# wq in four strided transfers, output in four transfers, x loaded later, filler matmuls, and GpSimd closing: a change at the two ends of a stream-bound decode kernel

## The chip, the cores and the metric

The kernel runs on one core of a Trainium2 chip. Times are device microseconds (us) of that core. "Before" was timed again beside every kernel, on the same chip.

The span of a profile, from the first to the last instruction, is 1.8 us shorter than the time of the same execution (988.36 us against 990.17).

## The reference

Decode attention with a cache of 4096 keys, followed by a gated feed-forward network:

```
x: (4, 1, 640) bf16
k_cache, v_cache: (4, 32, 4096, 192)       201 MB each: nearly all the bytes
h   = x + Attn(layernorm(x)) @ wo          q = layernorm(x) @ wq, wq: (640, 6144)
out = h + (silu(ln(h) @ w_gate) * (ln(h) @ w_up)) @ w_down
```

## The kernel before

SyncE (SP) issues all the loads, from one queue: wq first, then the k and v slots in turn as slots come free, then wo, w_gate, w_up and w_down. An issue is the instruction by which an engine's queue starts a transfer; a transfer has landed with the last update of its semaphore that the trace shows (the 16th for wq here). The parts that matter here are the first and the last instructions (cuts marked with `...`):

```python
xd = dma("act", lambda e: e.dma_start(x16[:, :], x[:, 0, :].rearrange("b (n d) -> (b n) d", n=4)), S_x)
...
wq_land = dma("sp", lambda e: e.dma_start(            # 128 partitions x 61,440 B
    wqsb[:, :, :].rearrange("q c n -> q (c n)"), wq[:, :].rearrange("(q c) n -> q (c n)", c=CD)), S_wq)
...
load_k(0); load_k(1)
for u in range(NU):
    load_v(u)
    if u + 2 < NU: load_k(u + 2)
...
for c in range(CF):                                   # w_down, three transfers: c 0-5, 6-9, 10-11
    for n in range(4):
        a = op("pe", lambda e, c=c, n=n: e.matmul(
            psH[32 * n:32 * n + 32, 0:DQ], lhsT=guT[:, c, :], rhs=wdsb[:, c, n * DQ:(n + 1) * DQ],
            start=False, stop=(c == CF - 1), skip_group_check=True), [gut, wd_land[c], ln2])
a = op("dve", lambda e: e.tensor_copy(out=outsb[:, 0:DQ], in_=psH[:, 0:DQ]), [a])
fin = [dma(eng, lambda e, n=n: e.dma_start(           # two transfers of 8 rows of 320 B
    out[:, 0, n * DQ:(n + 2) * DQ].rearrange("b (n d) -> n b d", n=2),
    outsb[32 * n:32 * n + 64:RB, 0:DQ]), S_out, [a]) for n, eng in ((0, "sp"), (2, "act"))]
with nc.Block(no_gpsimd_drain=True) as block:
    pr.emit(block, "act", fin[-1:])                   # ACT waits for both
```

The result sits in 16 of 128 partitions, every eighth one (`RB` is 8).

## Time and profile before

| | before |
|---|---|
| time, median of 6 | 990.44 us (990.21 to 990.85) |
| span of the profile | 988.4 us |
| read from memory | 424.29 MB, 429 GB/s over the span |
| first bulk packets of the 16 DMA engines | 1.76 to 3.21 us, mean 2.22 |
| last w_down piece landed | 985.01 us (its first engine 983.36) |
| output issue starts, output landed, end | 985.92, 987.88, 988.36 us |

From the page of before: its span, the granted TensorE clock and DMA share in 40 slices (tenths, 9 is 90% or more), GB/s by slice, the bytes, and the chain of waits.

```profile
span 988.4 us, 9462 instructions
...
PEclk9788778887777888777788777778877778877776
DMA  9999999999999999999999999999999999999997
GB/s 403 426 440 424 438 436 428 436 430 436 436 428 438 430 434 436 428 438 432 432 436 428 438 432 432 436 428 438 432 432 436 428 438 434 430 436 428 440 429 327
...
HBM read 424.29 MB, written 0.01 MB: 429 GB/s over the span
## 4 chain that ended last, share of the span: by engine, by line
DMA 67%; PE 18%; DVE 12%; issue 1%; SPq 1%; DVEq 0%
```

The DMA row is full in every slice but the last. In the packet records a row of 61,440 B takes 2.267 us on one DMA engine: 27.1 GB/s, 434 GB/s for 16. Only the first and last slices (403 and 327 GB/s) have anything to give.

In the timelines PE is TensorE, PEld its weight loads, DVE VectorE and ACT ScalarE; SPq and ACTq are the queues of SP and ACT, and x2 marks two instructions shown as one line. SP's timeline of before at the start (start, duration, queue, line, transfer):

```profile
0.74 0.39 SPq L331 DMA_DIRECT2D wq_sb<-in_A_wq_dram  x1
1.20 0.41 SPq L355 DMA_DIRECT2D k<-in_A_k_cache_dram  x1
```

The timeline of before at the end, all engines:

```profile
984.28 0.40 PEld L573 LDWEIGHTS pb<-wd_sb,guT 128*32 128x32 bf16 x16 [0.81 <-DMA wd_sb<-in_B_w_down_dram]
984.28 1.24 PE L573 MATMUL pb<-wd_sb,guT 128*32 128x160 bf16 x24 [0.49 <-DMA wd_sb<-in_B_w_down_dram]
985.06 0.14 PEld L573 LDWEIGHTS pb<-wd_sb,guT 128*32 128x32 bf16 x8 [0.38 <-DMA wd_sb<-in_B_w_down_dram]
985.57 0.33 DVE L576 CAST gu<-pb 128x160 bf16<-128x160 f32 x1 [2.86 <-PE pb L573]
985.92 0.68 SPq L577 DMA_DIRECT2D out_dram<-gu  x1
985.92 1.38 ACTq L577 DMA_DIRECT2D out_dram<-gu  x1
```

The last weights land at 985.01. Eight matmuls, a copy and two output issues follow, and the program ends 2.44 us after the output issue starts. Nothing is streamed in that tail (0 GB/s from 985 to 987 us), so whatever ends last there counts in full. The output issues last 0.68 us on SP and 1.38 on ACT.

### The profile page before, as it was taken

How to read it: one execution, taken by the hardware profiler on the slowest of the kernel's cores; microseconds unless marked ns; L12 is line 12 of the kernel's file. 1: busy time of each engine (PE TensorE's matmuls, PEld its weight loads, DVE VectorE, ACT ScalarE, POOL GpSimd, SP SyncE). 2: the span in 40 equal slices, each digit the busy share in tenths (PEclk: the TensorE clock that was granted, in tenths of full speed). 3: DMA queues.
4: the chain of work that ended last, by engine and by line, in shares of the span. 5: the costliest groups of instructions: out<-in, count | busy, mean ns of one | idle time of the engine just before them, and what ended most of it. 6: DMA issues, size and time to landing. Idle time of an engine off the chain costs nothing.

```text
span 988.4 us, 9462 instructions
## 1 busy us (share of the span) xinstructions
PE 581.5 (59%) x4409; PEld 128.6 (13%) x2941; DVE 552.6 (56%) x447; ACT 117.1 (12%) x376; POOL 3.6 (0%) x18
## 2 busy tenths in 40 slices
PE   1777555676555567545556654546765555675554
PEld 0001011111011111001111110111110111110023
DVE  1487545566655556655556665555666555566521
ACT  0311111100111110111111011111001111101120
POOL 1000000000000000000000000000000000000000
PEclk9788778887777888777788777778877778877776
DMA  9999999999999999999999999999999999999997
GB/s 403 426 440 424 438 436 428 436 430 436 436 428 438 430 434 436 428 438 432 432 436 428 438 432 432 436 428 438 432 432 436 428 438 434 430 436 428 440 429 327
DMA packets 10571, 424.39 MB, mean 429 GB/s; under 512 B 1220, under 2 KB 1220, under 8 KB 1732
## 3 DMA queue, kind: packets, MB, share of 16 engines
q1 hardware_dynamic: 10522, 424.29, 99.5%
q8 instruction: 5, 0.08, 0.0%
q10 hardware_dynamic: 42, 0.01, 0.0%
q14 instruction: 2, 0.02, 0.0%
HBM read 424.29 MB, written 0.01 MB: 429 GB/s over the span
## 4 chain that ended last, share of the span: by engine, by line
DMA 67%; PE 18%; DVE 12%; issue 1%; SPq 1%; DVEq 0%
DMA k<-in_A_k_cache_dram 64%; DVE prod L413 12%; PE pb L161 11%; PE pb L463 4%; DMA wd_sb<-in_B_w_down_dram 4%; PE pb L421 2%; SPq L366 0%; DVE sc L426 0%; PE pb L469 0%; DVEq L413 0%; SPq L392 0%; SPq L386 0%; PE pb L573 0%; PE pb L435 0%; SPq L331 0%
## 5 line engine op out<-in xcount | busy, mean ns | idle before, releaser
L413 DVE TENSOR_TENSOR prod<-k,qball 128x6144 f16<-128x6144 bf16 x128 | 426.4, 3352 | 220.1 <-DMA k<-in_A_k_cache_dram 220.1
L161 PE MATMUL pb<-prod,identH 128*128 128x512 f16 x1408 | 386.0, 431 | 0.0
L421 PE MATMUL pb<-prod,identH 128*128 128x512 f16 x128 | 57.9, 452 | 337.5 <-DVE prod L413 337.5
L426 DVE TENSOR_REDUCE sc<-pb 128x32 f32<-128x512 f32 x128 | 88.1, 688 | 108.7 <-PE pb L161 108.7
L478 ACT ACTIVATE otmp<-pb,minv 128x192 f32<-128x192 f32 x32 | 13.5, 421 | 649.1 <-PE pb L463 649.1
L421 PEld LDWEIGHTS pb<-prod,identH 128*128 128x128 f16 x128 | 13.2, 103 | 585.3 <-DVE prod L413 472.4
L463 PE MATMUL pb<-v,pbuf 128*8 128x384 bf16 x1984 | 86.0, 326 | 0.0
L454 ACT ACTIVATE pbuf<-sc,negM 32x128 bf16<-32x128 f32 x128 | 73.4, 574 | 4.9
L463 PEld LDWEIGHTS pb<-v,pbuf 128*8 128x8 bf16 x1984 | 45.4, 86 | 28.8
L482 DVE SCALAR_TENSOR_TENSOR orow<-pb,minv,otmp 128x192 f32<-128x192 f32 x32 | 13.4, 418 | 53.7 <-ACT otmp L478 53.7
L498 PEld LDWEIGHTS pb<-orow,here 128*128 128x128 f32 x256 | 33.5, 191 | 73.5 <-issue 71.1
L498 PE MATMUL pb<-orow,here 128*128 128x48 f32 x256 | 31.7, 267 | 1.1 <-DVE orow L482 1.1
L454 ACT ACTIVATION_READ_ACCUMULATOR pbuf<-sc,negM 32x1 f32 x128 | 31.8, 248 | 0.0
L448 ACT ACTIVATE negM<-pb 128x4 f32<-128x4 f32 x32 | 5.6, 174 | 160.2 <-PE pb L444 160.2
L469 PEld LDWEIGHTS pb<-lsb,headm 128*128 128x128 f32 x64 | 12.3, 194 | 74.8 <-issue 71.1
L444 PE MATMUL pb<-negMc,ones_row 1*128 1x4 f32 x64 | 12.2, 258 | 11.8 <-DVE negMc L439 11.8
L435 PE MATMUL pb<-identF,msb 128*1 128x128 f32 x64 | 12.1, 271 | 9.8 <-DVE msb L431 9.8
L439 DVE TENSOR_REDUCE negMc<-pb 1x4 f32<-1x128 f32 x32 | 8.9, 278 | 15.1 <-PE pb L435 15.1
L444 PEld LDWEIGHTS pb<-negMc,ones_row 1*128 1x128 f32 x64 | 9.4, 182 | 21.2 <-DVE negMc L439 21.2
L469 PE MATMUL pb<-lsb,headm 128*128 128x1 f32 x64 | 9.2, 213 | 2.7 <-ACT pbuf L454 2.7
L491 ACT ACTIVATE here<-place 128x131 f32 (+1 forms) x32 | 10.0, 312 | 0.9
L338 PE MATMUL pb<-wq_sb,lnT 128*32 128x384 bf16 x20 | 2.7, 520 | 12.1 <-DMA wq_sb<-in_A_wq_dram 12.1
(65 smaller groups left out, 91.1 us busy)
## 6 DMA issues: line engine op xcount, KB each, us to landing
k<-in_A_k_cache_dram SPq DMA_DIRECT2D x32, 6144.0 KB, 39.5
v<-in_A_v_cache_dram SPq DMA_DIRECT2D x31, 6144.0 KB, 25.5
wq_sb<-in_A_wq_dram SPq DMA_DIRECT2D x1, 7680.0 KB, 21.5
k<-in_A_v_cache_dram SPq DMA_DIRECT2D x1, 6144.0 KB, 39.8
wo_sb<-in_A_wo_dram SPq DMA_DIRECT2D x1, 5760.0 KB, 24.1
wo_sb<-in_A_wo_dram SPq DMA_DIRECT2D x1, 1920.0 KB, 26.1
wg_sb<-in_B_w_gate_dram SPq DMA_DIRECT2D x1, 1920.0 KB, 30.3
wu_sb<-in_B_w_up_dram SPq DMA_DIRECT2D x1, 1152.0 KB, 32.6
```

What stands on the lines that cost most here:

```text
L161: return e.add_instruction(mybir.InstMatmult(name=e.bass.get_next_instruction_name(), engine=mybir.EngineType.PE, start_tensor_calc=start, ...
L413: op("dve", lambda e: e.tensor_tensor(out=prod[BUF[k]][:, :, :], in0=kslot[u % 2][:, k * QT:(k + 1) * QT, :], in1=qball[:, bass.ds(u + pr. ...
L421: op("pe", lambda e, j=j: (e.matmul if j == 0 else partial(held_matmul, e))(psR[k][:, 0:QT * R], lhsT=identH[:, :], rhs=prod[BUF[k]][:, :, ...
L426: op("dve", lambda e: e.tensor_reduce(sc[u % 2][:, k * QT:(k + 1) * QT], psR[k][:, 0:QT * R].rearrange("q (t r) -> q t r", r=R), AX.X, ALU ...
L435: op("pe", lambda e: e.matmul(psS[0:1, XT], lhsT=msb[:, 0:1], rhs=identF[:, :], start=True, stop=True), [g("rmax", u), g("negM", u - 1), p ...
L444: op("pe", lambda e: e.matmul(psS[:, XB], lhsT=ones_row[0:1, :], rhs=negMc[0:1, :], start=True, stop=True), [g("hmax", u), g("negM", u - 1 ...
L454: op("act", lambda e, h=h, r=r: e.activation(out=pbuf[r, :, h], in_=sc[u % 2][r, :], func=ACTF.Exp, bias=negM[r, h:h + 1], scale=alpha, ac ...
L463: op("pe", lambda e, t=t, n=n: e.matmul(psO[32 * n:32 * n + 8, 0:2 * DH], lhsT=pbuf[:, t:t + 2, :].rearrange("q t m -> q (t m)"), rhs=vsrc ...
L469: op("pe", lambda e: e.matmul(psS[:, XL], lhsT=headm[:, :, :].rearrange("q r m -> q (r m)"), rhs=lsb[:, :], start=True, stop=True), [g("ex ...
L478: op("act", lambda e: e.activation(out=otmp[:, :], in_=psO[:, 0:DH], func=ACTF.Copy, scale=minv[:, 0:1]), [g("pv", u), g("minv", u), g("st ...
L482: op("dve", lambda e: e.scalar_tensor_tensor(out=orow[:, :], in0=psO[:, DH:2 * DH], scalar=minv[:, 1:2], in1=otmp[:, :], op0=ALU.mult, op1 ...
L498: op("pe", lambda e, i=i: e.matmul(psT[:, bass.ds(JW * at_unit(u)[0], JW)], lhsT=here[:, NI - 1 - i:NI - 1 - i + 128], rhs=orow[:, JW * i: ...
```

## The change

The intent was to give every DMA engine rows from the first issue (four transfers of every fourth partition), keep x's small load out of the way at the start, keep the TensorE clock up by filler matmuls, write the output by four plain transfers, and let idle GpSimd do the closing wait.

```diff
-    xd = dma("act", ..., S_x)
+    xd = dma("act", ..., S_x, [lambda: c2])               # c2: the identity is built
-    wq_land = dma("sp", lambda e: e.dma_start(
-        wqsb[:, :, :].rearrange("q c n -> q (c n)"), wq[:, :].rearrange("(q c) n -> q (c n)", c=CD)), S_wq)
+    for i in range(4):
+        wq_land = dma("sp", lambda e, i=i: e.dma_start(
+            wqsb[i:128:4, :, :].rearrange("q c n -> q (c n)"),
+            wq[:, :].rearrange("(q c) n -> q (c n)", c=CD)[i:128:4, :]), S_wq)
+    def idle(n):                                          # n matmuls 128x256 into an unused bank
...
+    idle(3) after w_gate, idle(2) inside w_up, idle(6) after w_up, idle(3) before w_down c = 6
-    fin = [... two transfers "n b d" of 8 rows, SP and ACT ...]
+    fin = [dma("sp" if n < 2 else "act", lambda e, n=n: e.dma_start(
+        out[:, 0, n * DQ:(n + 1) * DQ], outsb[32 * n:32 * n + 32:RB, 0:DQ]), S_out, [a]) for n in range(4)]
-        pr.emit(block, "act", fin[-1:])
+        pr.emit(block, "pool", fin[-1:])
```

(The `idle` lines stand for calls in the loops; the fin line removed is abridged.)

More of the change, by code (lines that the diff above doesn't have):

```diff
@@ L270, in g @@
         return tk[key] if key[1] >= 0 else None
-    xd = dma("act", lambda e: e.dma_start(x16[:, :], x[:, 0, :].rearrange("b (n d) -> (b n) d", n=4)), S_x)
+    xd = dma("act", lambda e: e.dma_start(x16[:, :], x[:, 0, :].rearrange("b (n d) -> (b n) d", n=4)), S_x, [lambda: c2])
     c1 = op("pool", lambda e: e.memset(r32[:, :], 0.0))
@@ L559, in build_kernel @@
     ln2 = layer_norm(psH[:, 0:DQ], [wo_done])
+    def idle(n):
+        for _ in range(n):
+            op("pe", lambda e: e.matmul(PB[2][:, 0:256], lhsT=sel[:, 0, :], rhs=sel[:, 0:2, :].rearrange("q b m -> q (b m)"),
+                                        start=True, stop=True), [tk["rsum", NU - 1, NQ - 1]])
     for k, w in enumerate((wgsb, wusb)):
         for c in range(CD):
+            if c == 3 and k == 1:
+                idle(2)
             for n in range(4):
@@ L565, in build_kernel @@
                     start=(c == 0), stop=(c == CD - 1)), [ln2, wu_land[c] if k else wg_land, g("rsum", u, NQ - 1)])
+        idle(6 if k else 3)
         if k == 0:
@@ L571, in build_kernel @@
     for c in range(CF):
+        if c == 6:
+            idle(3)
         for n in range(4):
@@ L576, in build_kernel @@
     a = op("dve", lambda e: e.tensor_copy(out=outsb[:, 0:DQ], in_=psH[:, 0:DQ]), [a])
-    fin = [dma(eng, lambda e, n=n: e.dma_start(
-        out[:, 0, n * DQ:(n + 2) * DQ].rearrange("b (n d) -> n b d", n=2),
-        outsb[32 * n:32 * n + 64:RB, 0:DQ]), S_out, [a]) for n, eng in ((0, "sp"), (2, "act"))]
+    fin = [dma("sp" if n < 2 else "act", lambda e, n=n: e.dma_start(
+        out[:, 0, n * DQ:(n + 1) * DQ], outsb[32 * n:32 * n + 32:RB, 0:DQ]), S_out, [a]) for n in range(4)]
     with nc.Block(no_gpsimd_drain=True) as block:
-        pr.emit(block, "act", fin[-1:])
+        pr.emit(block, "pool", fin[-1:])
     eg.close()
```

## The prediction

> **What bounds the kernel.** Memory traffic. The page gives 424.29 MB read in a span of 988.4 us (429 GB/s), with the DMA row at 9 tenths in all but the last slice. Packet by packet, an engine moves 61,440 B in 2.267 us, 27.1 GB/s, or 434 GB/s for 16. [...] The chain of waits is 67% DMA; the DVE and PE pieces on it run under transfers already queued. The change moves no byte less, so it can act only at the two ends: before the 16 engines stream (0 to about 3.2 us) and after the last weight has landed (985.01 to 988.36).
>
> **wq in four.** In the packet records the wq issue starts at 0.74 us; the first packets start at 1.76 to 1.91 us on eight engines, but at 2.26 to 2.76 on seven and at 3.21 on one, which an instruction fetch of 16 KB held (1.91 to 3.19). This skew is carried to the end: the 16 landings of the last w_down piece spread from 983.36 to 985.01. With 32 partitions per transfer, each engine gets two rows from the first issue, so all should start sooner: the seven perhaps 0.3 to 0.7 us earlier. The fetch stays. As the last engine decides (late ones are late by instruction fetches of about 1 us too), I book 0.4 us, possibly nothing. Three more issues on SP cost 0.4 us each, under queued data: nothing.
>
> **x later.** Issued at about 3.1 instead of 0.75 us. Before, it landed at 8.36 us because its packets queued behind rows of wq; afterwards at about 8.5 to 10. Layer norm ends 3.8 us later, and wq lands only at about 22: slack of 8 us or more. [...]
>
> **Idle matmuls.** The granted clock falls to 0.5 at 977.1 us. [...] the trace's clock steps are multiples of 3.41 us. If the fillers keep it at 1.0, only what follows a landing gains: the last eight w_down matmuls run from 985.06 to 985.52, perhaps 0.15 to 0.2 us less. The rest waits for weights in any case (up's second half for the landing at 980.27, w_down c=6 for 984.24). [...]
>
> **Output and closing.** Before: SP's issue takes 0.68, ACT's 1.38 us, first packets at 987.19 and 987.46, landed 987.88. Four plain issues should take about 0.4 each, as x's did (0.41), two in a row per engine: landed about 987.7, gain 0.15 (from a gain of 0.4 to a loss of 0.3, if issues serialize). GpSimd closing removes ACT's branch, drain and semaphore hop (987.91 to 988.12): 0.15.
>
> **Sum.** 0.4 + 0.15 + 0.15 + 0.15, about 0.9 us of 990.31: 989.4 us, range 988.5 to 990.2. Within 2%: 0.99.
>
> **What would show each step.** First wq packets of all engines before about 2.3 us except the one fetching; landings of k0 earlier by about 0.4 (36.79 before); the last w_down landing near 984.6; clock 1.0 after 977 us, and the last eight matmuls under 0.35 us; last output landing within 2.8 us of the last DVE copy's start; end at most 0.35 us after that landing.
>
> **What would make it wrong.** The longer PE program shifts or adds an instruction fetch in the tail, which holds one DMA engine for about 1 us; four output issues serialize; the gate stays at 0.5 and the fillers run into w_down's c=6; or the descriptor work of four transfers is no faster, and the start doesn't move. Runs of before already spread by 0.6 us.

## The result

| | before | changed |
|---|---|---|
| time, median of 6 | 990.44 us (990.21 to 990.85) | 991.73 us (991.55 to 992.36) |
| span of the profile | 988.36 | 989.76 |
| mean start of the 16 engines' first bulk packets | 2.22 us | 2.42 us |
| last w_down landing, last of 16 (mean of 16) | 985.01 (984.16) | 985.26 (984.43) |
| output issue starts | 985.92 | 986.16 |
| output landed, after that start | 1.96 | 3.23 |
| end, after that landing | 0.47 | 0.37 |

The ratio of the times is 1.0014, 95% interval 1.0001 to 1.0026. Ratios are the mean time of one kernel's fast runs over that of the other's of the same job, so not quite the ratio of the medians quoted. The change lost about 1.3 us where I had booked a gain of 0.9.

The page of changed, the lines that answer to those of before:

```profile
span 989.8 us, 9494 instructions
...
PEclk9888778887777888777788877788887778887787
DMA  9999999999999999999999999999999999999997
GB/s 390 437 436 425 440 429 431 443 425 433 435 429 439 429 431 443 425 433 435 429 439 429 429 443 423 437 433 429 441 427 431 441 425 437 433 429 441 425 426 315
...
HBM read 424.29 MB, written 0.01 MB: 429 GB/s over the span
## 4 chain that ended last, share of the span: by engine, by line
DMA 66%; PE 19%; DVE 12%; issue 1%; SPq 1%; DVEq 0%
```

The middle is the same; the first slice fell from 403 to 390 GB/s, the last from 327 to 315. Both ends became worse. SP's timeline of changed at the start:

```profile
0.74 3.33 SPq L332 DMA_DIRECT2D wq_sb<-in_A_wq_dram  x4
4.11 0.59 SPq L357 DMA_DIRECT2D k<-in_A_k_cache_dram  x1
```

The timeline of changed at the end:

```profile
984.74 0.40 PEld L585 LDWEIGHTS pb<-wd_sb,guT 128*32 128x32 bf16 x16 [0.41 <-DMA wd_sb<-in_B_w_down_dram]
984.74 1.02 PE L585 MATMUL pb<-wd_sb,guT 128*32 128x160 bf16 x24
985.30 0.14 PEld L585 LDWEIGHTS pb<-wd_sb,guT 128*32 128x32 bf16 x8 [0.16 <-DMA wd_sb<-in_B_w_down_dram]
985.81 0.32 DVE L588 CAST gu<-pb 128x160 bf16<-128x160 f32 x1 [3.11 <-PE pb L585]
986.16 1.82 SPq L589 DMA_DIRECT2D out_dram<-gu  x2
986.16 2.08 ACTq L589 DMA_DIRECT2D out_dram<-gu  x2
```

The last two lines are the main loss: each queue now spends about 2 us on issuing. The sum closes, in us of the two profiles: issue start +0.24, issue to landing +1.27, landing to end -0.10, together +1.41 (span 988.355 to 989.761). The single issues and packets, from the instruction and packet records of the traces (not a view of the page):

```
                  issue start + duration                        first packet of each issue
before   SP  985.918 + 0.679                                    987.19
         ACT 985.923 + 1.382                                    987.46
changed  SP  986.160 + 0.739, then 987.344 + 0.636              987.50, 988.62
         ACT 986.165 + 1.446, then 987.645 + 0.596              987.77, 988.98
wq issues, before:  0.738 + 0.392                               first packet 1.76
wq issues, changed: 0.738 + 0.597, 1.395 + 0.563, 2.001 + 1.433, 3.477 + 0.595   first packet 2.12
```

The first issue of each queue got no shorter with 4 rows instead of 8 (0.74 and 1.45 us against 0.68 and 1.38), the second adds 0.64 and 0.60, and its packets start 1.1 to 1.2 us after the first's. The trace of changed shows 20 updates of the output's semaphore for four transfers of 4 rows: for each, one ahead of its first packet and four that follow data. Before's two show 6: for each, one ahead and two that follow data. Each update that follows data goes with one packet of 4 B behind the rows, which I read as one DMA engine: four a transfer instead of two. So the four-way form did spread over more engines, but a row's packet takes 0.02 us; there was nothing to spread.

### The profile page after: what moved, and what is told of

The parts are those of the page before. It is cut to its first block, busy times and chain, and to the rows that moved or that the text cites. A ratio compares the mean times of both kernels' runs of the same rounds, so it can differ in the third digit from the quotient of the medians.

```text
span 989.8 us, 9494 instructions
## 1 busy us (share of the span) xinstructions
PE 579.7 (59%) x4422; PEld 128.9 (13%) x2955; DVE 552.5 (56%) x447; ACT 117.1 (12%) x376; POOL 3.6 (0%) x18
## 4 chain that ended last, share of the span: by engine, by line
DMA 66%; PE 19%; DVE 12%; issue 1%; SPq 1%; DVEq 0%
DMA k<-in_A_k_cache_dram 62%; PE pb L161 12%; DVE prod L415 12%; PE pb L465 4%; DMA wd_sb<-in_B_w_down_dram 4%; PE pb L423 2%; SPq L368 0%; DVE sc L428 0%; SPq L332 0%; PE pb L585 0%; PE pb L471 0%; DVEq L415 0%; SPq L388 0%; PE pb L564 0%; PE pb L437 0%
## 5 line engine op out<-in xcount | busy, mean ns | idle before, releaser
L433 DVE TENSOR_REDUCE msb<-sc 128x1 f32<-128x128 f32 x32 | 9.2, 286 | 1.1
```

## The experiments

All edits below are against the kernel before unless they say "changed kernel". Where a timing is given as a difference, it is mean against mean of one job. There is one profile of each run, so a duration is only as good as its repeats. At the end of the program they are good: the output landed 1.96 to 1.98 us after its issue starts in all six profiles that keep before's two output transfers, and 3.23 to 3.24 in all three that have both the wq split of the change and four output transfers. The landing of the last weights is not: in the eleven undisturbed profiles without a split (out1_sp_pool's first is left out, see there) the last of its 16 parts lands anywhere from 984.90 to 985.63 us. So for it I use the mean of the 16 parts (984.00 to 984.16 in these).

### d_out4: the four output transfers alone

```diff
-    fin = [... two transfers ...]
+    fin = [dma("sp" if n < 2 else "act", ... four transfers ...) for n in range(4)]
```

> The kernel before with only the output in four transfers (ACT still closes). Theory O (the output issues made the loss: the second issue of each queue starts about 1.2 us after the first, so the last output lands later): about +1.25 us in time, last output landing 3.2 us after the first output issue starts instead of 1.96; first bulk packets and the last w_down landing as before. Rival (the loss is made at the start by the wq split, and the tail of after only looks longer by chance): within 0.3 us of before.

Measured: 991.22 us beside 990.55 (means +0.78); ratio 1.0008, interval 0.9995 to 1.0022. Output landed 2.97 us after its issue starts (before 1.96), the end 3.44 us after it (2.44). Timeline, the output's lines:

```profile
985.80 1.39 SPq L577 DMA_DIRECT2D out_dram<-gu  x2
985.81 1.90 ACTq L577 DMA_DIRECT2D out_dram<-gu  x2
```

The tail grew by 1.0 us with nothing else changed, so the output issues are the larger part of the loss. It is less than the 1.25 us expected: here SP's second issue follows the first at once (0.05 us), so that its 1.82 us of issuing became 1.39, and ACT's, whose second transfer lands last, 1.90 instead of 2.08.

### undo_out: the changed kernel with before's output

```diff
-    fin = [dma("sp" if n < 2 else "act", ... four ...) for n in range(4)]
+    fin = [... two transfers as before ...]
```

> The changed kernel with the output of before (two transfers), everything else kept. Theory O: about 1.25 us faster than the changed kernel, so about +0.1 us against before (start +0.25, closing by GpSimd -0.1 to -0.15). Rival (start makes the loss): still +1 us or more.

Measured: 990.51 us beside 990.55, means +0.01; ratio 1.0, interval 0.9986 to 1.0013. Issue to end 2.33 us. Without its output, the changed kernel loses nothing that the times can show. Timeline, the output's lines:

```profile
986.36 0.67 SPq L589 DMA_DIRECT2D out_dram<-gu  x1
986.36 1.38 ACTq L589 DMA_DIRECT2D out_dram<-gu  x1
```

### a_wq_strided and wq_blocks: the wq split, with and without stepped partitions

```diff
+            wqsb[i:128:4, ...],            wq...[i:128:4, :]                 # a_wq_strided, as in the change
+            wqsb[32 * i:32 * i + 32, ...], wq...[32 * i:32 * i + 32, :]      # wq_blocks
```

> The kernel before with only wq in four transfers of every fourth partition. Theory S (a transfer whose partitions are stepped takes longer to issue, about 0.6 instead of 0.39 us, and its first packets leave about 0.35 us later): first bulk packets at about 2.1 us, last w_down landing +0.2 to +0.3 us, time +0.25 us. Rival (the late x load shifted the start, not the split): first packets at 1.76 us and the landing unchanged or earlier.

> The kernel before with wq in four transfers of 32 consecutive partitions each. Theory S (stepping costs): each issue takes about 0.39 us, first packets at 1.76 us, last w_down landing earlier than before by up to 0.4 us. Rival S2 (a split into smaller transfers costs, whatever the partitions): issue of about 0.6 us and first packets at about 2.1 us again, landing +0.2 us.

Measured, a_wq_strided: 990.69 us beside 990.55 (means +0.16); ratio 1.0002, interval 0.9988 to 1.0016. First issue 0.58 us, first packet at 2.09 us, as theory S has it. The last w_down landing, 985.28 (+0.27), proves little, as profiles without the split reach 985.63; the mean of its 16 parts is the surer measure: 984.37, and 984.37 to 984.43 in all five profiles with this split, against 984.00 to 984.16 without. The time alone doesn't resolve it.

wq_blocks: issues of 0.41, 0.40 and 0.42 us (the third took 1.18), first packet at 1.77 us. So smaller transfers are not slower to issue; stepping by four partitions is, in this load (the slow third issue comes with either form of split: 1.18 here, 1.35 to 1.67 stepped). The slowness reaches the issue behind it: k's, with 128 neighbouring partitions, took 0.59 to 0.60 us right after stepped ones and 0.43 after these blocks. But the mean of the 16 first packets stayed at 2.18 us with the latest at 3.09, so even quick issues of fewer rows did not remove the skew of the engines that the split was meant to remove.

And the kernel took 1010.24 us, ratio 1.0199, interval 1.0185 to 1.0213, which neither theory expected. The window view over 4 to 20 us, first of wq_blocks, then of changed (last two columns: DMA share and GB/s):

```profile
4.00:20.00 16.00, 0.88 (x3) 0.60 (x3) 2.35 (x10) 0.29 (x1) 1.18 (x5) 1.00 0.92 188
```

```profile
4.00:20.00 16.00, 0.88 (x3) 0.60 (x3) 2.35 (x10) 1.12 (x2) 1.19 (x5) 1.00 1.00 430
```

Each row of 61,440 B took 4.79 us instead of 2.27, and wq landed at 41.98 us instead of 22.27: 19.7 us, the whole of the loss. In changed, with every fourth partition, a row took the usual 2.27 us. Why 32 neighbouring partitions lose a factor of 2.1 the runs do not show. So of the two splits tried only the stepped one keeps the rate, and stepping costs 0.2 us per issue and 0.35 us at the first packet.

### out1_sp and out1_act: the output in one transfer

```diff
-    fin = [... two transfers ...]
+    fin = [dma("sp", lambda e: e.dma_start(     # "act" in out1_act
+        out[:, 0, :].rearrange("b (n d) -> n b d", n=4), outsb[0:128:RB, 0:DQ]), S_out, [a])]
```

> The kernel before with the output in one transfer of 16 rows on SP (ACT closes, issues nothing). Theory O (the tail costs by issues, not by rows): SP's issue about 0.7 us, last landing about 1.7 us after the issue starts instead of 1.96, time -0.2 to -0.3 us. Rival R (descriptor work goes by rows): issue and first packet grow with 16 rows against 8, landing 2.2 us or later.

> The same one transfer, but on ACT. Theory C (ACT's first output issue takes 1.38 us because it contends with SP's, which starts at the same moment): alone it takes about 0.7 us and lands as in the run on SP. Rival F (ACT's first issue after a millisecond is slow by itself): 1.3 us or more again, landing about 2.0 us or later.

Measured: out1_sp 990.24 and out1_act 990.35 us beside 990.44, means -0.25 each; both ratios 0.9998, interval 0.9984 to 1.0012. Both landed 1.77 us after the issue starts (before 1.96). Timeline lines of out1_sp, then out1_act:

```profile
986.00 0.70 SPq L577 DMA_DIRECT2D out_dram<-gu  x1
```

```profile
985.87 1.13 ACTq L577 DMA_DIRECT2D out_dram<-gu  x1
```

Sixteen rows cost an issue no more than eight or four: 0.70, 0.68 and 0.74 us on SP. From 4 to 16 rows, this tail goes by issues, not by rows. On ACT the one issue still takes 1.13 us without SP beside it, so neither theory C nor F is right as stated: about 0.25 of the 1.38 us go with SP's issue beside it, most is there alone. It doesn't delay the packets: both kernels' leave 1.3 us after the issue starts.

### out2_sp: both of before's output transfers on SP

```diff
-    ... for n, eng in ((0, "sp"), (2, "act"))]
+    ... for n, eng in ((0, "sp"), (2, "sp"))]
```

> The two output transfers of before, both on SP. Theory Q (a further issue waits on its own queue until the one ahead is through, about 0.7 us): second packets 0.7 us after the first, last landing 2.4 to 2.5 us after the issue starts instead of 1.96, time +0.45 us. Rival G (one generator serves both queues, so it doesn't matter which queue issues): landing 1.96 us, as before.

Measured: 990.87 us beside 990.68, means +0.16; ratio 1.0002, interval 0.9988 to 1.0015. Packets 0.61 us after the first issue's, last landing 2.31 us after the issue starts: +0.35, near theory Q's 0.45, and not G's zero. Timeline line:

```profile
986.29 1.24 SPq L577 DMA_DIRECT2D out_dram<-gu  x2
```

Against all 16 rows in one transfer (1.77 us), two transfers land 0.54 us later on one queue and 0.2 us later on two: the second queue hides about two thirds of the second issue's cost.

### out_rows_wrong and warm_out1: why does an output issue take 0.7 us?

```diff
-        outsb[32 * n:32 * n + 64:RB, 0:DQ]    # out_rows_wrong: neighbouring rows, wrong values on purpose
+        outsb[32 * n:32 * n + 8, 0:DQ]
```
```diff
+    warm = dma("sp", lambda e: e.dma_start(x16[:, :], ... x ...), S_x, [gut])   # warm_out1, with one output transfer
```

> Wrong on purpose: the two output transfers of before read eight neighbouring partitions each instead of every eighth, so the values are wrong, the bytes and the shape the same. Theory S (stepped partitions make an issue slower, as with wq): SP's issue 0.45 instead of 0.68 us, first packets about 1.0 instead of 1.27 us after the issue starts, last landing about 1.6 to 1.7 instead of 1.96 us. Rival (the output issue is slow because it writes to memory, or because the queue had been quiet): no change.

> The kernel before with the output in one transfer on SP, and a dummy load of x (nothing reads it) issued on SP 3 us ahead of it. Theory W (an output issue is slow because its queue had been quiet for 38 us): SP's output issue about 0.45 instead of 0.70 us, first packets about 1.0 instead of 1.3 us after it starts, landing 1.5 us instead of 1.77. Rival D (a store from SBUF is slow to issue by itself): 0.65 to 0.7, 1.3 and 1.77 us as without the dummy; the dummy load itself shows whether a load after the quiet takes 0.4 us.

Measured: out_rows_wrong (values wrong) 990.77 us beside 990.68, ratio 1.0, interval 0.9987 to 1.0014. Its SP issue took 0.77 us, not 0.45 (timeline line below), and it landed 2.06 us after the start. My theory that stepped partitions slow the output as they slow wq fell.

```profile
986.54 0.77 SPq L577 DMA_DIRECT2D out_dram<-gu  x1
```

warm_out1, timeline:

```profile
983.13 0.34 SPq L577 DMA_DIRECT2D x<-in_A_x_dram  x1
...
986.24 0.70 SPq L578 DMA_DIRECT2D out_dram<-gu  x1
```

After 35 us of quiet, a load of 16 rows took 0.34 us to issue, and the store of 16 rows 2.8 us later still took 0.70 and landed in 1.78 us. So the quiet queue is not the cause either. (990.33 us beside 990.53; ratio 0.9999, interval 0.9985 to 1.0012.) What remains is that these stores from SBUF are slow to issue by themselves. Whether that is their direction is not shown. They differ from the loads in one more way, which I did not test: each uses only 2 or 4 DMA engines, read from the updates of the semaphore (3 or 5 a transfer, one of them ahead of the data), while the loads here, the dummy load of x too, use all 16 (16 updates a transfer). No run has a store on 16 engines or a load on fewer.

### undo_wq, after_again and wq_out4: why the parts don't add up

The whole lost 1.3 us, the output alone 0.78 and the split alone 0.16.

```diff
 undo_wq      changed kernel, wq in one transfer
 after_again  changed kernel
 wq_out4      before, wq in four strided transfers and the output in four
```

> The changed kernel with wq back in one transfer. The output alone cost +0.7 us in time, and the changed kernel lost 1.3, though without its output it lost nothing: 0.5 us come from the parts together. Theory P (SP's longer program, three more issues, moves its second output issue; it started 0.45 us after the first had ended, with 0.05 in the run of the output alone): gap back to 0.05 us, output landing 2.97 us after its issue instead of 3.23, time about 0.5 us less than the changed kernel. Rival (the gap comes from something else, chance or the GpSimd wait): gap 0.45 us again, time less by at most 0.2 us.

> The changed kernel once more, beside the parts on one chip. If the gap of 0.45 us ahead of SP's second output issue belongs to the kernel, it is there again, output landing 3.2 us after its issue, time +1.2 to +1.4 us; if it was chance, gap 0.05 us, landing 3.0 to 3.15 us, time +1.0 us.

> The kernel before with the wq split and the four output transfers, without late x, fillers and GpSimd's closing. Theory P (SP's three more issues bring the gap): gap 0.45 us, output landing 3.2 us after its issue, time +1.2 us or more. Rival (the fillers or the closing bring it): gap 0.05 us, landing 3.0 us, time +0.95 us, the sum of the two parts alone (0.78 + 0.16 in means).

| | time beside before | means | ratio (interval) | gap ahead of SP's second output issue | output landed after its issue starts |
|---|---|---|---|---|---|
| d_out4 | 991.22 / 990.55 | +0.78 | 1.0008 (0.9995 to 1.0022) | 0.05 | 2.97 |
| undo_wq | 991.27 / 990.44 | +0.87 | 1.0009 (0.9995 to 1.0023) | 0.05 | 3.13 |
| after_again | 991.95 / 990.53 | +1.36 | 1.0014 (1.0001 to 1.0028) | 0.45 | 3.23 |
| wq_out4 | 992.14 / 990.53 | +1.58 | 1.0016 (1.0003 to 1.0030) | 0.45 | 3.24 |

wq_out4's timeline, the output's lines (d_out4's are above: 1.39 and 1.90):

```profile
986.40 1.82 SPq L579 DMA_DIRECT2D out_dram<-gu  x2
986.41 2.08 ACTq L579 DMA_DIRECT2D out_dram<-gu  x2
```

Theory P holds for the gap: it is there in every trace that has both the split and the four output transfers, and in none that has the four transfers without the split; late x, fillers and closing don't bring it. The instruction records of the other traces go further: in all six profiles of kernels with three more wq issues, wq_blocks too, SP takes up whatever follows its first output issue 0.44 to 0.45 us after that issue has ended, even where only the end of the program follows (a_wq_strided, undo_out, wq_blocks); in the eleven other profiles in which SP issues output it is 0.05 us, with one output issue or two. So the gap belongs to the three issues more, stepped or not, and not to the four stores; it costs time only when a second output issue stands behind it. The two parts together account for the whole loss. What in SP's longer program makes SP wait, I did not settle. P was wrong in one number: without the gap undo_wq still landed in 3.13 us rather than 2.97, because ACT's first issue took 1.44 us as in changed, not 1.28 as in d_out4. The gap explains about 0.1 to 0.27 us; the other 0.4 to 0.5 us of the difference between +1.58 and 0.78 + 0.16 I leave unassigned. The means of five runs are no surer than about 0.2 us (the changed kernel in two jobs: +1.34 and +1.36; wq_out4 +1.58, though it differs from it only by small parts), and the last weights, ahead of the tail, scatter by up to 0.7 us from profile to profile.

### e_pool and c_idle: the closing and the fillers alone

```diff
-        pr.emit(block, "act", fin[-1:])
+        pr.emit(block, "pool", fin[-1:])      # e_pool; c_idle has only the idle() calls of the change
```

> The kernel before with GpSimd closing alone. From the last output landing to the end 0.37 us instead of 0.475, so -0.1 us; within the scatter of the times.

> The kernel before with the filler matmuls alone. Theory I ([...] the fillers keep the clock up at the end only by luck; all they can win is about 0.14 us, and at half clock they cost nothing because the last landing still decides): time within 0.2 us of before, last landing to last DVE copy between 0.42 us (clock 1.0 there) and 0.56 us (clock 0.5). Rival (fillers at half clock delay the w_down matmuls): last landing to copy 0.6 us or more, time +0.2 us or more.

Measured, e_pool: 990.24 us beside 990.44, means -0.29; ratio 0.9997, interval 0.9983 to 1.0011. Landing to end 0.37 us, against 0.47: the profile shows -0.10, the rest is scatter.

c_idle: 990.48 us beside 990.68, means -0.12; ratio 1.0, interval 0.9986 to 1.0013. Last landing to last copy 0.42 us, against 0.56. Window view of c_idle, then of changed, around the last matmuls (the column after the busy times, before the DMA share, is the granted clock):

```profile
984.00:986.00 2.00, 1.41 (x35) 0.60 (x27) 0.26 (x1) 0.00 (x0) 0.00 (x0) 0.95 0.06 23
```

```profile
983.00:986.20 3.20, 2.70 (x51) 1.52 (x51) 0.32 (x1) 0.00 (x0) 0.00 (x0) 0.51 0.29 114
```

In c_idle the clock was up when the last eight matmuls ran; in the first profile of changed it fell at 983.07 us, and there the fillers won nothing. The times between the clock's steps are multiples of 3.41 us in before and changed (before's last steps: 956.66, 960.08, 970.32 and 977.14 us). Over all profiles with fillers, four of five show 0.41 to 0.43 us from landing to copy (undo_out, undo_wq, c_idle, after_again) and one 0.55; all thirteen without fillers show 0.55 or 0.56. So it is less luck than I expected: 0.13 us, most of the time. The fillers do not keep the clock up, though. In all five profiles with them it falls to 0.5 at 975.0 to 977.4 us and comes back to 1.0 once: in four of them at 982.38 to 985.20 us, so that all or most of the last eight matmuls run at 1.0, in the first of changed too early (979.66 to 983.07). In the thirteen without fillers it had been at 0.5 for 8 us or more when these matmuls started.

### out1_sp_pool, twice: a version that should beat both

```diff
 one output transfer on SP (as out1_sp), GpSimd closes (as e_pool)
```

> One output transfer of 16 rows on SP, and GpSimd closes: the two parts that gained in their own traces. From the output issue to the end 2.1 us (before 2.44; the one transfer alone 2.23, GpSimd alone 2.33), time about -0.3 us: 990.1 to 990.2 us beside 990.4 to 990.5. If the parts don't add, 2.2 us or more.

> The same kernel as out1_sp_pool, whose profile fell on an execution with the last weights 1.9 us late. Its tail was 2.14 us, 0.3 us less than before's 2.44. Expected here: tail 2.1 to 2.15 us again, time 0.2 to 0.4 us less than before on the same chip, if no such execution comes.

The first time 990.57 us beside 990.68, ratio 0.9998, interval 0.9984 to 1.0011: inconclusive. One execution of five took 991.79 us, and it was the profiled one; its last weights landed at 986.94 us, 1.9 us late, before the tail began. I did not find what held them. Its tail, 2.14 us, was as expected. The second time 990.09 us (990.04 to 990.25) beside 990.53, means -0.42; ratio 0.9996, interval 0.9982 to 1.0010. Issue to end 2.15 us, against before's 2.44. Each part's gain is plain in the profiles (0.19 of landing, 0.10 of closing); as a time, the interval still holds 1. It is the best version seen, by about 0.3 us of 990.

## Why the prediction was wrong

It gave 989.4 us (988.5 to 990.2); measured 991.73.

1. **What bounds the kernel, and where the change can act**: right. The stream was the same 429 GB/s, and every difference lay in the first 4 and the last 5 us.
2. **Output: the step that failed.** "Four plain issues should take about 0.4 each, as x's did (0.41), two in a row per engine: landed about 987.7, gain 0.15". They took 0.74 and 0.64 on SP, 1.45 and 0.60 on ACT; the output landed 3.23 us after the issue starts instead of 1.96: a loss of 1.27, four times the worst I allowed. I took a load's duration for a store. The trace of before already showed two stores at 0.68 and 1.38, and I put that down to their two-level pattern. out1_sp (16 rows in a two-level pattern, 0.70) and the change (4 plain rows, 0.74) show that a plain pattern issues no faster; warm_out1 shows load and store beside each other, 0.34 and 0.70 (why the store is slower stays open, see there).
3. **wq in four**: the sign was wrong. Booked: 0.4 us gained, because all engines would start sooner. Measured: mean first packet 2.42 instead of 2.22 us; the mean landing of the last w_down piece was 984.37 to 984.43 us in the five profiles with the split and 984.00 to 984.16 in the eleven undisturbed ones without: about 0.3 us later. How much of it reaches the end the times don't resolve (+0.16 in a_wq_strided alone). "Three more issues on SP cost 0.4 us each" was 0.56 to 1.43: stepped partitions issue slower (0.56 to 0.60 against 0.40 to 0.42 in wq_blocks), and the third took longer in either form, which no run explains. That they cost nothing "under queued data" held for the stream: k0, issued at 4.11 instead of 1.20 us, landed at 36.66 us (36.79). But they brought the gap of 0.44 us behind SP's first output issue, which with the four stores cost another 0.1 to 0.27 us at the end. I had no such term.
4. **x later**: right. It landed at 8.73 us (8.36 before), in the range given, far ahead of wq at 22.1. undo_wq, which keeps it, starts its packets at 1.75 us. It was not run alone.
5. **Fillers**: the size (0.15 us) was right in four of five profiles; the first profile of changed was the fifth. The mechanism, that fillers keep the clock at 1.0, was my assumption and only half right: the clock was not kept at 1.0 after 977 us in any of them, but came back in time for the last matmuls in four.
6. **GpSimd closing**: right; booked 0.15, measured 0.10 us.

The signs that the prediction named for its steps did not appear either: first wq packets ran to 3.10 us and not 2.3, k0 landed 0.12 us earlier and not 0.4, the last w_down piece at 985.26 and not near 984.6, the last output 3.58 us after the last DVE copy's start and not 2.8, the end 0.37 us after that and not 0.35.

The range was too narrow because I treated the worst case of the output, "if issues serialize", as 0.3 us. Two durations of before's own profile, 0.68 and 1.38, were the ones to add.

## What to carry to other kernels

In a tail where nothing streams, count issues, not rows (here a row's packet took 0.02 us, a first output issue on SP 0.67 to 0.77): take the duration of the same kind of transfer (store or load, as many DMA engines, the same issuing engine) from the trace, and write a small result with one transfer rather than several (landed 1.77 us after the issue starts here, against 1.96 with two and 2.97 with four). Don't split the first load of a stream to start it sooner without checking the packets: here the issue got slower with stepped partitions (0.58 us instead of 0.39), groups of 32 neighbouring partitions halved the rate (4.79 us a row instead of 2.27), and three added issues brought a gap of 0.44 us at the other end of the program. When several small changes are made at once, run the pairs too: here two parts that lost 0.16 and 0.78 us alone lost 1.58 together.

## Durations that these traces show

- From issue to first packet: counted from the end of SP's issue 0.59 to 0.64 us, loads of neighbouring partitions and stores alike; from its start 0.99 to 1.03 us for a load and 1.27 to 1.37 for a store. The issue itself: loads 0.33 to 0.45 us (neighbouring partitions, and not right behind a stepped one), these stores 0.67 to 0.77 on SP and 1.13 to 1.48 on ACT for the first one.
- For a last transfer of a few KB the issues are a large part of the tail: both output transfers on SP landed in 2.31 us, on two queues in 1.96, as one transfer in 1.77.
- A load with stepped partitions took longer to issue: 0.56 to 0.60 us against 0.40 to 0.42 for as many neighbouring ones, first packet at 2.1 against 1.77 us.
- With 32 neighbouring partitions a transfer a row took 4.79 us, with 32 stepped ones 2.27.
- An instruction fetch of 16 KB among the packets of a full stream took about 1 us (five fetches in each profile: the first 0.95 to 2.33 us, the later ones 0.88 to 1.08).
